# Linear attention into a two-layer network: k's maxima from a second copy of k with heads on the partitions, spread through DRAM

## The chip, the cores and the metric

The kernel runs on one core of one Trainium2 chip. The metric is the device time of one execution in microseconds (us). The engines are PE (TensorE, matmuls), ACT (ScalarE), DVE (VectorE), POOL (GpSimd) and SP (SyncE, which issues all DMAs here). Each works through its own instructions in order and waits for the others by semaphores.

## The reference

q, k and v have the shape 8 (batch) x 8 (heads) x 576 (positions) x 64. k's softmax runs over the positions, q's over the 64 elements of a row; the result, 4608 rows of 512, goes through a network with a hidden width of 2048. All is float32.

```python
q_s = np.exp(q - np.max(q, axis=-1, keepdims=True))
q_s = q_s / (np.sum(q_s, axis=-1, keepdims=True) + 1e-09)
k_s = np.exp(k - np.max(k, axis=2, keepdims=True))
k_s = k_s / (np.sum(k_s, axis=2, keepdims=True) + 1e-09)
kv = np.einsum('bhsd,bhse->bhde', k_s, v)
attn = np.einsum('bhsd,bhde->bhse', q_s, kv)
...
h = x @ w_in
g = np.where(h >= 1, h, np.where(h <= -1, 0.0, (h + 1) ** 2 / 4))
return g @ w_out
```

## The kernel before, in words

**Tiling.** The 4608 rows are worked in nine chunks of 512 rows (c); batch b's k and v are prepared in the stage of the same number. Heads go in four pairs (pr) of 2 x 64 = 128; two pairs make a half (h). The hidden width is cut into 16 blocks of 128 (f). A main matmul multiplies 128 x 128 weights with 128 x 512; each product of the network is three of them, from high and low parts of both factors. The first layer (h, L1446) runs block by block for chunks 0 to 2; chunks 3 to 8 go two at a time through seven products for four blocks (hA, hb, hC, L1505). The second layer (o, L1659) adds into one PSUM bank for each quarter of the chunk's rows. Between the two, ACT and DVE form g (relu L1596, square L1600, minimum L1605) and its parts gh (L1643) and gl (L1648).

**Attention.** Batches 0 and 1 (function attention) read k with the heads' elements on the partitions (in_kt, tiles kt or k of 128 x 576), so that a maximum over positions is one reduction along the free axis (L952). Batches 2 to 7 (attention_two, both halves: twelve stages) read k with positions on the partitions (in_k, 128 x 5 x 128), as kv_mms needs it. There the maximum runs across partitions:

- k_max (L1213): DVE reduces each pair's five rows per partition to m, 128 x 128, one per pair
- k_tr (L1221): PE transposes m into the tile mt in PSUM bank a, twice
- k_top (L1227): DVE reduces the two transposed tiles to mx, 128 x 2
- k_spread (L1232): PE transposes each column of mx, broadcast, back into mt, so that each partition holds all 128 maxima, twice
- k_sub (L1242): DVE subtracts mt from k; bank a is held until here
- k_exp (L1248) on ACT, then kv_mms (L1258), 40 matmuls on PE, kv_z and kv_f, which leave k's normalised product with v in kvt. x_two (L839) multiplies the transposed q with kvt to form the chunk's x.

**Order.** The kernel does not issue work as it is written. Each operation is noted in a plan with its engine, an estimated duration, a due time and what it waits for; tile buffers are handed on by rings, in which a taker waits until the earlier tile's readers are done. k's tiles have two rooms (for half 0 the tag k, for half 1 the tag st1). Plan.settle makes a first order by due times, then tries random moves of operations, one for each number in TURNS, and keeps an order unless Plan.play, a model of the engines with those durations, says that it is longer. The instructions are then recorded in that order, each on its engine. Loads and stores share SP's queue, in which a load that waits for a store's landing holds what stands behind it.

Of the kernel before, what the change touches and what calls it, by code (L numbers as in the profile page):

```python
# [13 lines left out]
F32 = mybir.dt.float32  # L14
# [64 lines left out]
class Op:  # L79
# [4 lines left out]
    def __init__(self, engine, us, due, emit, deps, port, kb, slack, other=()):  # L84
        self.engine, self.us, self.due, self.emit = engine, us, due, emit
        self.port, self.kb, self.slack = port, kb, slack
        self.ways = ((engine, us, port), *other)
        self.deps, self.users = deps, []
        self.missing = len(deps)
        self.ready = self.after = 0.0  # L90
        self.store = False
        self.margin = 0.8 if kb else 0.0
        self.wire = kb / 330
        for d in deps:
            d.users.append(self)
# [19 lines left out]
class Plan:  # L115
# [79 lines left out]
    )  # L195

    CASES, LATE = 3, 1.6

# [288 lines left out]
def tile_linear_attention_then_ffn(  # L487
# [414 lines left out]
    def attention(c, pr, due, step, slack):  # L902
# [163 lines left out]
        if not first:  # L1066
            rpk.take(mm)
# [842 lines left out]
```

## Time and profile before

| | us |
|---|---|
| three timed runs | 845.15, 844.44, 845.61 |
| median | 845.15 |
| the profiled execution's own time | 844.76 |
| its span, from the first to the last instruction | 843.0 |
| PE busy in it | 828.4 |
| first main matmul starts | 20.65 |

The profile is of one execution. A row of a group gives line, engine, operation, output <- inputs, shapes, count, then the busy time of the group, the mean duration in ns of one instruction, and the idle time of the engine just before them with what ended it. PEld are PE's weight loads, which overlap its matmuls. A DMA row gives the issues, the size of one and the median time from issue to landing. In the timeline and the chain the first two columns are start and duration.

### The profile page before, as it was taken

To read this page: it belongs to the slowest core of one execution; us is meant where nothing else is said; L and a number is where in the kernel's file an instruction comes from. 1 tells how busy PE (TensorE), PEld (TensorE's weight loads), DVE (VectorE), ACT (ScalarE), POOL (GpSimd) and SP (SyncE) were. 2 spreads that over 40 slices of the span, in tenths; PEclk is the share of its full clock that TensorE was granted. 3 is DMA by queue.
4 is the path that set the end of the run, shared out by engine and by line. 5 is a ranking of instruction groups with operands and counts; after the bars stand their busy time and mean duration, and the time that the engine had idled before them with its cause. 6 is when DMAs were issued, how large, how long until landed. Compare 5 with 4: busy or idle time off the path is not lost.

```text
span 843.0 us, 12228 instructions
## 1 busy us (share of the span) xinstructions
PE 828.4 (98%) x4364; PEld 663.6 (79%) x4364; DVE 457.3 (54%) x853; ACT 442.5 (52%) x758; POOL 329.1 (39%) x291
## 2 busy tenths in 40 slices
PE   8899999999999999999999999999999999999998
PEld 6587778877777787877877888787778888888786
DVE  6887774566756656776754315765641034545300
ACT  6787756443466454644656445554574245444522
POOL 4664555552446756200217691102157600000153
PEclk9999999999999999999999999999999999999999
DMA  9898865457578566766675536556465254544232
GB/s 338 274 318 294 290 218 213 145 165 241 193 258 274 173 217 224 246 215 228 194 248 206 153 99 194 195 193 210 145 216 178 76 187 138 175 138 162 75 102 87
DMA packets 65580, 166.38 MB, mean 197 GB/s; under 512 B 7280, under 2 KB 7536, under 8 KB 65520
## 3 DMA queue, kind: packets, MB, share of 16 engines
q1 hardware_dynamic: 65520, 165.61, 58.7%
q8 instruction: 34, 0.56, 0.3%
q14 instruction: 26, 0.21, 0.1%
HBM read 122.06 MB, written 43.52 MB: 196 GB/s over the span
## 4 chain that ended last, share of the span: by engine, by line
PE 93%; DVE 2%; ACT 2%; issue 1%; POOL 1%; DMA 1%; POOLq 0%; ACTq 0%
PE o L1659 45%; PE h L1446 16%; PE hA L1505 15%; PE hC L1505 8%; PE hb L1505 4%; PE x L839 2%; PE kv L1258 2%; PE warm L1841 1%; PE kv L988 1%; DMA out<-osb 1%; DVE qmo L1345 0%; ACT r L1596 0%; PE ep L963 0%; ACT osb L533 0%; PE tp L1035 0%
## 5 line engine op out<-in xcount | busy, mean ns | idle before, releaser
L1659 PE MATMUL o<-wl,gh 128*128 128x512 f32 x576 | 227.8, 396 | 0.3 <-ACT osb L533 0.3
L1659 PE MATMUL o<-wh,gl 128*128 128x512 f32 x576 | 224.9, 390 | 0.1
L1659 PE MATMUL o<-wh,gh 128*128 128x512 f32 x576 | 224.4, 390 | 0.0
L1505 PE MATMUL hA<-x,w 128*128 128x512 f32 x576 | 145.8, 392 | 1.6 <-ACT sn_P L533 1.2
L1659 PEld LDWEIGHTS o<-wl,gh 128*128 128x128 f32 x576 | 108.1, 188 | 26.8 <-issue 3.6
L1659 PEld LDWEIGHTS o<-wh,gl 128*128 128x128 f32 x576 | 108.1, 188 | 24.9 <-POOL gl L1648 1.0
L1505 PEld LDWEIGHTS hA<-x,w 128*128 128x128 f32 x576 | 107.2, 188 | 26.0 <-ACT sn_P L533 1.8
L1659 PEld LDWEIGHTS o<-wh,gh 128*128 128x128 f32 x576 | 108.2, 188 | 21.4
L1446 PE MATMUL h<-x,w 128*128 128x512 f32 x432 | 110.1, 396 | 2.2 <-DVE gl L1648 1.5
L1446 PEld LDWEIGHTS h<-x,w 128*128 128x128 f32 x432 | 79.3, 188 | 23.0 <-DVE gl L1648 2.1
L1600 ACT ACTIVATE r<-r 128x512 f32<-128x512 f32 x139 | 87.8, 633 | 3.8
L1505 PE MATMUL hC<-x,w 128*128 128x512 f32 x288 | 73.9, 392 | 0.1
L1596 ACT ACTIVATE r<-c,half 128x512 f32<-128x512 f32 x48 | 34.7, 723 | 68.2 <-DVE c L1529 68.1
L1648 POOL TENSOR_TENSOR gl<-gs,gh 128x512 fp32r<-128x512 f32 x42 | 54.2, 1291 | 41.7 <-ACT gh L1643 41.1
L1354 POOL TENSOR_TENSOR q<-q,qzb 128x512 f32<-128x512 f32 x28 | 28.9, 1050 | 105.3 <-DVE qzb L1376 91.0
L1354 POOL TENSOR_TENSOR q<-q,qmb 128x512 f32<-128x512 f32 x28 | 28.8, 1049 | 100.9 <-DVE qmb L1346 100.9
L1154 POOL TENSOR_TENSOR x<-xc,x 128x512 fp32r<-128x512 f32 x40 | 51.8, 1307 | 35.9 <-ACT x L1149 35.9
L1643 ACT CAST gh<-gs 128x512 fp32r<-128x512 f32 x42 | 26.1, 622 | 73.2 <-PE o L1659 63.4
L1505 PEld LDWEIGHTS hC<-x,w 128*128 128x128 f32 x288 | 53.6, 188 | 12.3 <-DVE sn_P L535 0.5
L1596 ACT ACTIVATE r<-h,half 128x512 f32<-128x512 f32 x48 | 33.0, 687 | 52.2 <-PE h L1446 51.9
L1648 POOL TENSOR_TENSOR gl<-c,gh 128x512 fp32r<-128x512 f32 x6 | 7.8, 1294 | 126.9 <-ACT gh L1643 126.8
L1605 DVE SCALAR_TENSOR_TENSOR h<-h,r 128x512 f32<-128x512 f32 x48 | 33.1, 694 | 37.1 <-ACT r L1600 34.0
(123 smaller groups left out, 1176.3 us busy)
## 6 DMA issues: line engine op xcount, KB each, us to landing
w<-b SPq DMA_DIRECT2D x50, 512.0 KB, 4.5
w<-s SPq DMA_DIRECT2D x48, 512.0 KB, 3.5
st<-in_w SPq DMA_DIRECT2D x32, 512.0 KB, 6.2
g<-c SPq DMA_DIRECT2D x42, 256.0 KB, 4.1
gs<-g SPq DMA_DIRECT2D x42, 256.0 KB, 2.6
v<-in_v SPq DMA_DIRECT2D x32, 325.0 KB, 4.9
q<-in_q SPq DMA_DIRECT2D x36, 256.0 KB, 3.7
out<-osb SPq DMA_DIRECT2D x35, 256.0 KB, 2.5
```

The lines of the kernel that those rows point to most:

```text
L839: nc.tensor.matmul(t[r][cols, :, p0:p1], kvt[rows, g % NKV, pr, :], q[pr]["tq"][rows, :, p0:p1], start=True, stop=True, tile_position=(r * ...
L1154: eng.tensor_tensor(x[:, 1, :], t["xc"][:, at, :], f32(x[:, 0, :]), ALU.subtract)
L1258: nc.tensor.matmul(kv[d, i, :], t[pr]["k"][:, j, d], t[pr]["v"][:, j, e * (D + 1) : (e + 1) * (D + 1)], start=(j == 0), stop=(j == KJ - 1) ...
L1354: nc.gpsimd.tensor_tensor(qf, qf, at, alu)
L1446: nc.tensor.matmul(t["h"], lhs, rhs, start=(turn == 0 and i == 0), stop=(turn == NPAIR - 1 and i == 2),)
L1505: nc.tensor.matmul(banks[b]["h"], lhs, rhs, start=(begins and not kk and not m), stop=(ends and kk == 1 and m == 2), skip_group_check=True,)
L1596: nc.scalar.activation(t["r"], t["h"], AF.Relu, bias=half[:, :1], scale=0.5)
L1600: nc.scalar.activation(t["r"], t["r"], AF.Square)
L1605: nc.vector.scalar_tensor_tensor(t["h"], t["h"], 1.0, t["r"], ALU.max, ALU.min)
L1643: nc.scalar.copy(t["gh"], t["h"])
L1648: eng.tensor_tensor(t["gl"], t["h"], f32(t["gh"]), ALU.subtract)
L1659: nc.tensor.matmul(outs[c, j], lhs[:, s], rhs, start=(begins and i == 0), stop=(closes and i == 2),)
```

## The change

In the twelve stages of attention_two the maxima of k come from a second copy of k. in_kt, which held batches 0 and 1, now holds all eight, in the layout with heads on the partitions. For each pair a stage loads its 128 x 576 copy into one of k's rooms, DVE reduces it along the free axis to a column of mx (128 x 2), and the copy's room is free again. mx is stored to a small DRAM tensor mk, 2 x 128, element by element, and loaded back as one row of 256 that goes to all 128 partitions of m2. k_sub subtracts this tile from k, which is loaded as before. k_tr, k_top and k_spread, with their four transposes on PE and the hold on PSUM bank a, are gone.

The planner gets a mode for each PE operation (0 main matmuls, 1 x_two, 2 the kv products, 3 transposes); its model adds 0.1 when the mode changes, and the estimates of x_two and kv_mms are lower by 0.1 and 0.09. The numbers in TURNS are others. Lines after the change are smaller by 16 to 22: L1483 stands for L1505, L1637 for L1659, L1234 for L1258.

```diff
     TURNS = (
-        10001, 10002, 10003, 10011, 10013, 10026, 10029, 10031, 10033, 10036, 10041, 10042,
...
+        2, 3, 4, 12, 18, 19, 20, 21, 25, 27, 30, 31, 34, 35, 37, 39, 41, 43, 44, 46, 47, 49, 51,
...
+            if e == "PE" and op.mode != mode:
+                t, mode = t + 0.1, op.mode
...
-        xm = do("PE", 1.05, due, x_mm, *ready, *deps)
+        xm = do("PE", 0.95, due, x_mm, *ready, *deps)
+        xm.mode = 1
...
         def k_max(i):
             def emit():
                 if not i:
-                    b["m"] = wk.tile([P, 2, P], F32, tag="m2", name=f"m2_{n}")
-                k = t[two[i]]["k"].rearrange("p j d -> p d j")
-                nc.vector.tensor_reduce(b["m"][:, i, :], k, AX.X, ALU.max)
...
+                    b["mx"] = sm.tile([P, 32], F32, tag="mx", name=f"mx_{n}", bufs=1)
+                kt_ = t[two[i]]["kt"].rearrange("p j s -> p (j s)")
+                nc.vector.tensor_reduce(b["mx"][:, i : i + 1], kt_, AX.X, ALU.max)
...
+        def m_store():
+            nc.sync.dma_start(maxima.rearrange("i p -> p i"), b["mx"][:, :2])
+
+        def m_load():
+            b["m"] = wk.tile([P, 2, P], F32, tag="m2", name=f"m2_{n}")
+            nc.sync.dma_start(
+                b["m"].rearrange("p i d -> p (i d)"),
+                maxima.rearrange("i p -> (i p)").unsqueeze(0).broadcast_to([P, 2 * P]),
+            )
...
-                mb = t[pr]["mb"].unsqueeze(1).broadcast_to([P, KJ, P])
+                mb = b["m"][:, pr % 2, :].unsqueeze(1).broadcast_to([P, KJ, P])
                 nc.vector.tensor_tensor(k, k, mb, ALU.subtract)
...
+            maxima = dp.tile([2, P], F32, name=f"mk{n}")
+            rx, rm = ring("sm mx", 1), ring("wk m2", 1)
+            tops, before = [], rx.wait()
             for i, pr in enumerate(two):
+                lk, rk = load(pr, "kt", kt[c, pr], [P, 1, S], 288, kdue - 14 + 3 * i, tag)
+                km = do("DVE", 0.75, kdue - 12 + 3 * i, k_max(i), lk, *before)
+                rk.free(km)
...
+            out_ = plan.save(0.45, kdue - 6, m_store, tops, 64)
+            rx.free(out_)
+            spread = plan.read(0.45, kdue - 2, m_load, [out_, *rm.wait()], 128)
+            rm.take(spread)
...
+                subs.append(do("DVE", 0.9, kdue + 14, k_sub(pr), lk, spread, port=True))
...
-            one = do("PE", 0.13, kdue + 8, k_tr(0), loads[two[0], "m"], *ra.wait())
-            ra.take(one)
-            other = do("PE", 0.13, kdue + 8, k_tr(1), loads[two[1], "m"], one)
-            top = do("DVE", 0.4, kdue + 10, k_top, one, other)
-            rm.free(top)
-            spread = [do("PE", 0.13, kdue + 12, k_spread(i), top) for i in range(2)]
-            subs = [do("DVE", 0.81, kdue + 14, k_sub(pr), *spread) for pr in two]
-            ra.free(*subs)
...
-            mm = do("PE", 1.34, at, kv_mms, *exps, *deps, *ra.wait())
+            mm = do("PE", 1.25, at, kv_mms, *exps, *deps, *ra.wait())
+            mm.mode = 2
```

Three places show how the instructions move; all belong to chunk 6, half 0. In a row stand line, operation, output <- inputs, shape and a repeat count; the last number in a name only counts tiles.

PE before, in the first products of chunks 3 and 4 (hb, hC) beside the last second-layer block of chunk 2 (o_2, block 15): the transposes are mt.

```order
L1505 MATMUL hb_3_0_3560<-x3_3517,w_3_0_0_3401 128x512 x3
L1659 MATMUL o_2_1_2749<-wl15_1030,gh_2_15_3525 128x512
L1659 MATMUL o_2_1_2749<-wh15_1029,gh_2_15_3525 128x512
L1659 MATMUL o_2_1_2749<-wh15_1029,gl_2_15_3536 128x512
L1221 MATMUL mt_6_0_3575<-ident_95,m2_6_0_3547 128x128 x2
L1505 MATMUL hC_3_0_3583<-x6_2973,w_3_0_1_3407 128x512 x3
L1505 MATMUL hC_3_0_3583<-x7_3549,w_3_0_1_3407 128x512 x3
L1659 MATMUL o_2_2_2740<-wl15_1030,gh_2_15_3525 128x512
L1659 MATMUL o_2_2_2740<-wh15_1029,gh_2_15_3525 128x512
L1659 MATMUL o_2_2_2740<-wh15_1029,gl_2_15_3536 128x512
L1232 MATMUL mt_6_0_3575<-ident_95,mx_6_0_3592 128x128 x2
L1659 MATMUL o_2_3_2764<-wl15_1030,gh_2_15_3525 128x512
```

PE now, at the same work:

```order
L1637 MATMUL o_2_1_2751<-wl15_1047,gh_2_15_3543 128x512
L1637 MATMUL o_2_1_2751<-wh15_1046,gh_2_15_3543 128x512
L1637 MATMUL o_2_1_2751<-wh15_1046,gl_2_15_3550 128x512
L1483 MATMUL hA_3_0_3578<-x0_2730,w_3_0_0_3469 128x512 x3
L1483 MATMUL hA_3_0_3578<-x1_3563,w_3_0_0_3469 128x512 x3
L1234 MATMUL kv_6_0_3592<-v_6_0_3341,k_6_0_3384 64x65 x10
L1234 MATMUL kv_6_0_3592<-v_6_1_3348,k_6_1_3402 64x65 x10
L1483 MATMUL hb_3_0_3622<-x2_2778,w_3_0_0_3469 128x512 x3
L1483 MATMUL hb_3_0_3622<-x3_3576,w_3_0_0_3469 128x512 x3
```

The two pairs of transposes are gone, and the kv products, which stood 14 rows behind the second pair before, now stand among these products.

DVE before, the same stage: L1213 are the maxima of k, L1227 k_top, L1242 the subtractions.

```order
L1213 TENSOR_REDUCE m2_6_0_3547<-k_6_0_3489 128x128
L1213 TENSOR_REDUCE m2_6_0_3547<-k_6_1_3493 128x128
L1529 TENSOR_TENSOR hb_3_0_3560<-hb_3_0_3560,sn_P1_3_0_3542 128x512
L1334 TENSOR_REDUCE qa_6_0_3436<-q_6_1_3498 128x16
L1227 TENSOR_REDUCE mx_6_0_3592<-mt_6_0_3575 128x2
L1605 SCALAR_TENSOR_TENSOR hb_3_0_3560<-hb_3_0_3560,r_3_0_3581 128x512
L535 COPY osb_2_1_3601<-o_2_1_2749 128x512
L1648 TENSOR_TENSOR gl_3_0_3613<-hb_3_0_3560,gh_3_0_3603 128x512
L1345 COPY qmo_6_0_3617<-qa_6_0_3436 32x32 x4
L1346 TENSOR_TENSOR qmb_6_0_3618<-qa_6_0_3436,qmo_6_0_3617 128x32
L1242 TENSOR_TENSOR k_6_0_3489<-k_6_0_3489,mt_6_0_3575 128x640
L1242 TENSOR_TENSOR k_6_1_3493<-k_6_1_3493,mt_6_0_3575 128x640
```

DVE now, from the second maximum (L1200) to what stands behind the subtractions (L1218); L1583 is the minimum, L1626 gl, L742 a split of summed weights:

```order
L1200 TENSOR_REDUCE mx_6_0_3376<-kt_6_1_3325 128x1
L1353 TENSOR_SCALAR qzb_5_0_3364<-qzb_5_0_3364 128x32
L1354 RECIPROCAL qzb_5_0_3364<-qzb_5_0_3364 128x32
L1583 SCALAR_TENSOR_TENSOR h_2_12_3397<-h_2_12_3397,r_2_12_3418 128x512
L1200 TENSOR_REDUCE mx_5_1_3439<-kt_5_2_2954 128x1
L1626 TENSOR_TENSOR gl_2_12_3449<-h_2_12_3397,gh_2_12_3441 128x512
L742 TENSOR_TENSOR w_s_7_0_3447<-ss_7_3420,w_s_7_0_3447 128x2x256
L1583 SCALAR_TENSOR_TENSOR h_2_13_3359<-h_2_13_3359,r_2_13_3432 128x512
L1218 TENSOR_TENSOR k_6_0_3384<-k_6_0_3384,m2_6_0_3426 128x640
L1218 TENSOR_TENSOR k_6_1_3402<-k_6_1_3402,m2_6_0_3426 128x640
L1583 SCALAR_TENSOR_TENSOR h_2_14_3353<-h_2_14_3353,r_2_14_3467 128x512
L1626 TENSOR_TENSOR gl_2_13_3503<-h_2_13_3359,gh_2_13_3496 128x512
```

The stage has moved ahead, to the last blocks of chunk 2; seven instructions now stand between the second maximum and the subtraction that waits for the load.

SP before, the stage's loads beside weight fetches (w_3) and stores (out):

```order
L1201 DMA k_6_0_3489<-in_k 128x640
L1201 DMA k_6_1_3493<-in_k 128x640
L1201 DMA q_6_1_3498<-in_q 128x512
L676 DMA w_3_0_3_3509<-b1_113 128x512
L1201 DMA v_6_0_3511<-in_v 128x650
L1201 DMA v_6_1_3519<-in_v 128x650
L1717 DMA out<-osb_2_0_3557 128x512
```

SP now, from the second copy's load; mk is the store of the maxima, m2 their load:

```order
L1188 DMA kt_6_1_3325<-in_kt 128x576
L658 DMA w_2_15_3336<-b15_127 128x1024
L1188 DMA v_6_0_3341<-in_v 128x650
L1188 DMA v_6_1_3348<-in_v 128x650
L1188 DMA k_6_0_3384<-in_k 128x640
L1205 DMA mk6_0_175<-mx_6_0_3376 128x2x1
L856 DMA xk4_3_173<-xo_4_3_3395 128x512
L1188 DMA k_6_1_3402<-in_k 128x640
L1209 DMA m2_6_0_3426<-mk6_0_175 128x256
L1188 DMA k_5_2_3451<-in_k 128x640
L750 DMA s7_0_142<-w_s_7_0_3447 128x1024
L658 DMA w_3_0_0_3469<-b0_112 128x1024
```

Between the store and the load of the maxima stand two other DMAs; the fetches of the next weights stand behind the load.

More of the change, by code (lines that the diff above doesn't have):

```diff
@@ L93, in __init__ @@
         self.wire = kb / 330
+        self.mode = 0
         for d in deps:
@@ L323, in play @@
         ends, gaps, why = {}, [], {}
+        mode = 0
         for op in order:
@@ L1052, in attention @@
         tr = do("PE", 0.6, 2, kt_tr, ke, *rpk.wait(), *(et.wait() * first))
+        tr.mode = 3
         rpk.take(tr)
@@ L1059, in attention @@
             tr = do("PE", 0.25, 2.7, kt_tr2, ke, *rpk.wait())
+            tr.mode = 3
             rk.free(tr)
@@ L1084, in attention @@
         tr = do("PE", 0.45, 3.6, q_tr, qn, *rpq.wait())
+        tr.mode = 3
         rpq.take(tr)
@@ L1210, in emit @@
                 if not i:
-                    b["m"] = wk.tile([P, 2, P], F32, tag="m2", name=f"m2_{n}")
-                k = t[two[i]]["k"].rearrange("p j d -> p d j")
-                nc.vector.tensor_reduce(b["m"][:, i, :], k, AX.X, ALU.max)
-            return emit
-        def k_tr(i):
-            def emit():
-                if not i:
-                    b["mt"] = ps_a.tile([P, 4, P], F32, tag="a", name=f"mt_{n}")
-                nc.tensor.transpose(b["mt"][:, i, :], b["m"][:, i, :], ident)
-            return emit
-        def k_top():
-            b["mx"] = sm.tile([P, 32], F32, tag="mx", name=f"mx_{n}", bufs=1)
-            nc.vector.tensor_reduce(b["mx"][:, :2], b["mt"][:, 0:2, :], AX.X, ALU.max)
-        def k_spread(i):
-            def emit():
-                t[two[i]]["mb"] = b["mt"][:, 2 + i, :]
-                nc.tensor.transpose(
-                    t[two[i]]["mb"], b["mx"][:, i : i + 1].broadcast_to([P, P]), ident
-                )
-            return emit
+                    b["mx"] = sm.tile([P, 32], F32, tag="mx", name=f"mx_{n}", bufs=1)
+                kt_ = t[two[i]]["kt"].rearrange("p j s -> p (j s)")
+                nc.vector.tensor_reduce(b["mx"][:, i : i + 1], kt_, AX.X, ALU.max)
+            return emit
+        def m_store():
[6 more added lines that the diff above has]
+            )
         def k_sub(pr):
@@ L1278, in attention_two @@
         if c < NB:
-            rm = ring("wk m2", 1)
-            loads, rooms, maxed = {}, {}, rm.wait()
-            for i, pr in enumerate(two):
-                tag = ("k", "st1")[h]
-                loads[pr, "k"], rooms[pr, "k"] = load(
-                    pr, "k", k[c - KT, pr], [P, KJ, P], 320, kdue + 6 * i, tag
+            loads, rooms = {}, {}
+            tag = ("k", "st1")[h]
+            maxima = dp.tile([2, P], F32, name=f"mk{n}")
+            rx, rm = ring("sm mx", 1), ring("wk m2", 1)
+            tops, before = [], rx.wait()
+            for i, pr in enumerate(two):
+                lk, rk = load(pr, "kt", kt[c, pr], [P, 1, S], 288, kdue - 14 + 3 * i, tag)
+                km = do("DVE", 0.75, kdue - 12 + 3 * i, k_max(i), lk, *before)
+                rk.free(km)
+                tops.append(km)
+                if not i:
+                    rx.take(km)
+                before = [km]
+            out_ = plan.save(0.45, kdue - 6, m_store, tops, 64)
+            rx.free(out_)
+            spread = plan.read(0.45, kdue - 2, m_load, [out_, *rm.wait()], 128)
+            rm.take(spread)
+            subs, exps = [], []
+            for i, pr in enumerate(two):
+                lk, rooms[pr, "k"] = load(
+                    pr, "k", k[c - KT, pr], [P, KJ, P], 320, kdue + 10 + 6 * i, tag
                 )
@@ L1288, in attention_two @@
                 )
-            for i, pr in enumerate(two):
-                km = do("DVE", 1.3, kdue + 6 * i, k_max(i), loads[pr, "k"], *maxed, port=True)
-                maxed = [km]
-                if not i:
-                    rm.take(km)
-                loads[pr, "m"] = km
-            exps = []
-            ra = ring("ps a", 1)
-            one = do("PE", 0.13, kdue + 8, k_tr(0), loads[two[0], "m"], *ra.wait())
-            ra.take(one)
-            other = do("PE", 0.13, kdue + 8, k_tr(1), loads[two[1], "m"], one)
-            top = do("DVE", 0.4, kdue + 10, k_top, one, other)
-            rm.free(top)
-            spread = [do("PE", 0.13, kdue + 12, k_spread(i), top) for i in range(2)]
-            subs = [do("DVE", 0.81, kdue + 14, k_sub(pr), *spread) for pr in two]
-            ra.free(*subs)
+                subs.append(do("DVE", 0.9, kdue + 14, k_sub(pr), lk, spread, port=True))
+            rm.free(*subs)
             exps = [do("ACT", 0.74, kdue + 20 + 12 * i, k_exp(pr), subs[i]) for i, pr in enumerate(two)]
@@ L1308, in attention_two @@
             deps = [loads[pr, "v"] for pr in two]
-            mm = do("PE", 1.34, at, kv_mms, *exps, *deps, *ra.wait())
+            mm = do("PE", 1.25, at, kv_mms, *exps, *deps, *ra.wait())
+            mm.mode = 2
             ra.take(mm)
@@ L1870 @@
     kk = rows(inputs["k"]).transpose(0, 1, 3, 4, 2, 5).reshape(b, NPAIR, P, 2 * KJ * D)
-    kt = rows(inputs["k"])[:KT].transpose(0, 1, 2, 5, 4, 3).reshape(KT, NPAIR, P, KJ * P)
+    kt = rows(inputs["k"]).transpose(0, 1, 2, 5, 4, 3).reshape(b, NPAIR, P, KJ * P)
     kt = kt[..., :S]
```

116 rows, old and new, of the table TURNS are left out of this document.

## The prediction

> **What bounds the kernel now.** I read the page first: its busy shares and its chain.
>
> ```profile
> span 843.0 us, 12228 instructions
> PE 828.4 (98%) x4364; PEld 663.6 (79%) x4364; DVE 457.3 (54%) x853; ACT 442.5 (52%) x758; POOL 329.1 (39%) x291
> ...
> PE 93%; DVE 2%; ACT 2%; issue 1%; POOL 1%; DMA 1%; POOLq 0%; ACTq 0%
> ```
>
> TensorE (PE) is busy in 98% of the span, and 93% of the chain that ended last is its work. The other engines stand idle 46% of the time or more. So a change is worth what it takes out of PE's row of instructions or out of PE's waits, and costs what it adds to either. Work on DVE, SP or the DMA engines counts only where PE comes to wait for it.
>
> Next the busy times by stage (start and end, length, PE busy with its count, then PEld, DVE, ACT, POOL, clock, DMA share, GB/s):
>
> ```profile
> 20.00:104.00 84.00, 80.36 (x436) 62.01 (x431) 66.90 (x122) 64.13 (x116) 48.95 (x39) 1.00 0.87 294
> 104.00:312.00 208.00, 205.82 (x1195) 164.22 (x1194) 129.94 (x260) 106.48 (x185) 111.09 (x107) 1.00 0.61 206
> 312.00:632.00 320.00, 317.77 (x1667) 253.57 (x1667) 185.81 (x344) 173.12 (x291) 108.16 (x92) 1.00 0.60 200
> ```
>
> The twelve stages that the change touches lie in the last two of these rows, and the clock stands at its full 1.00. PE idles there for 208.00 - 205.82 + 320.00 - 317.77 = 4.4 us in all. That is all that better timing could win there; the rest must come from fewer instructions. PE's waits between 95 and 570 us, where the twelve stages lie, all of them (total, times, longest):
>
> ```profile
> PE h L1446 <- DVE gl L1648: 1.5, 1, 1.5
> PE hA L1505 <- ACT sn_P L533: 1.2, 1, 1.2
> PE kv L1258 <- ACT k L1248: 0.9, 2, 0.7
> PE o L1659 <- ACT osb L533: 0.3, 1, 0.3
> ```
>
> One row is on the path that the change replaces: kv_mms waited 0.9 us for the exponential of k. No row names a DMA. That matters below, because the change moves the maxima from PE to DMAs.
>
> **What the transposes cost on PE.** They are these two groups, 48 instructions:
>
> ```profile
> L1221 PE MATMUL mt<-ident,m 128*128 128x128 f32 x24 | 4.9, 271 | 0.0
> L1232 PE MATMUL mt<-ident,mx 128*128 128x128 f32 x24 | 4.7, 272 | 0.0
> ```
>
> Their busy time is no price, since matmuls overlap in the pipeline; I take it from starts. An undisturbed run of main matmuls gives the step:
>
> ```profile
> 143.06 5.44 PE o L1659 x24
> ```
>
> 24 matmuls in 5.44 us, so 0.227 us from start to start. Now a pair of transposes in PE's timeline, and then one standing alone (start, duration):
>
> ```profile
> 117.69 1.53 PE L1446 MATMUL h<-x,w 128*128 128x512 f32 x6
> 119.06 0.38 PE L1221 MATMUL mt<-ident,m 128*128 128x128 f32 x2
> 119.19 0.48 PE L1659 MATMUL o<-wl,gh 128*128 128x512 f32 x1
> 119.51 0.39 PE L1659 MATMUL o<-wh,gh 128*128 128x512 f32 x1
> 119.74 0.40 PE L1659 MATMUL o<-wh,gl 128*128 128x512 f32 x1
> 119.97 0.85 PE L1446 MATMUL h<-x,x 128*128 128x512 f32 x3
> ...
> 153.78 0.85 PE L1446 MATMUL h<-x,x 128*128 128x512 f32 x3
> 154.46 0.27 PE L1221 MATMUL mt<-ident,m 128*128 128x128 f32 x1
> 154.49 0.94 PE L1446 MATMUL h<-x,w 128*128 128x512 f32 x3
> 155.27 0.85 PE L1446 MATMUL h<-x,x 128*128 128x512 f32 x3
> ```
>
> From 117.69 to 119.97 stand 6 + 3 = 9 main matmuls, which need 9 x 0.227 = 2.04 us; they took 2.28. The pair costs 0.24: about 0.14 before the next main matmul starts, and 0.09 because the one after it comes 0.32 instead of 0.227 later. From 153.78 to 155.27 stand 6 main matmuls, 1.36 us; they took 1.49, so a lone transpose costs 0.13. Part of the price is thus for leaving and re-entering the main matmuls, not for the transpose.
>
> **The change part by part.** *Transposes removed.* In the order before, the 48 stand as 21 pairs and 6 alone, each time between main matmuls; afterwards there are none. 21 x 0.24 + 6 x 0.13 = **5.8 us** off PE. Nothing hides this; PE is the engine that is never free.
>
> *Planner's mode count.* PE's main matmuls are interrupted in 72 places before and 44 after: 27 fewer by the transposes above, and one more because two remaining transposes now stand together. That one is worth the re-entry, 0.09: **0.1 us**. The new costs (1.25 for 1.34, 0.95 for 1.05) are numbers in the plan; the 20 matmuls per pair of heads, and all other PE work, stay.
>
> *DVE.* Rows for it:
>
> ```profile
> L1213 DVE TENSOR_REDUCE m<-k 128x128 f32<-128x640 f32 x24 | 30.8, 1302 | 0.0
> L1227 DVE TENSOR_REDUCE mx<-mt 128x2 f32<-128x256 f32 x12 | 5.1, 421 | 10.0 <-PE mt L1221 10.0
> L1242 DVE TENSOR_TENSOR k<-k,mt 128x640 f32<-128x640 f32 x24 | 18.7, 815 | 13.5 <-PE mt L1232 13.5
> L952 DVE TENSOR_REDUCE nm<-kt 128x1 f32<-128x576 f32 x4 | 2.9, 737 | 3.9 <-DMA kt<-in_kt 3.9
> ```
>
> The 24 maxima of k fall from 1.30 to about 0.74 each (the same reduction of the same shape in the last row): 30.8 - 17.8 = 13.0 us. The 12 second maxima go, 5.1 us. The subtraction keeps its shape, but its second operand moves from PSUM to SBUF. Operands of 128x512 take 0.692 us in the first row below (one in PSUM) and 0.687 in the second (both in SBUF), so I leave it at 0.815:
>
> ```profile
> L1529 DVE TENSOR_TENSOR c<-hC,sn_P 128x512 f32<-128x512 f32 x24 | 16.6, 692 | 52.1 <-PE hC L1505 48.3 <-ACT sn_P L533 2.8 <-ACT q L1361 1.1
> L1154 DVE TENSOR_TENSOR x<-xc,x 128x512 fp32r<-128x512 f32 x2 | 1.4, 687 | 2.7 <-ACT x L1149 2.7
> ```
>
> DVE loses 18 us of 457, worth nothing directly, since it was idle nearly half the time. For the kv wait it is worth between 0 and 0.9 us; I take **0.5**, half of that row, as the path is renewed and no row of it remains.
>
> *Loads added.* 24 loads of 288 KB and, with rows of 128 x 256, twelve of 128 KB: 8.4 MB more in the 528 us of two stages that move 206 and 200 GB/s, 107 MB: about 8%, or 5 points of their DMA share of 0.61 and 0.60. The copies take the rooms of k, two at a time, so each k is loaded only after a copy's maximum; its landing runs beside the round trip. The first six copies fall where the share is 0.87, before and just after 104 us. Cost 0 while PE waits for no DMA; if that cover went, each load ahead of a weight load would delay it by about 1 us (288 KB at 294 GB/s).
>
> *The wait added.* The maxima go to DRAM in pieces of 4 bytes and come back to all partitions; the load is issued on SP only when the store has landed. No such store is in the trace. The rows nearest to a store and a load by SP:
>
> ```profile
> xk<-xo SPq DMA_DIRECT2D x24, 256.0 KB, 4.0
> xc<-xk SPq DMA_DIRECT2D x24, 256.0 KB, 3.3
> ...
> b<-w SPq DMA_DIRECT2D x10, 512.0 KB, 6.9
> ...
> out<-osb SPq DMA_DIRECT2D x2, 128.0 KB, 2.0
> ```
>
> Low end of the round trip: twice the fastest row, 2.0 + 2.0 = 4.0 us. The closest pair by what it does is xk and xc, 4.0 + 3.3 = 7.3. High end: 6.9 + 3.3 = 10.2. I take 5.0, since 1 KB is stored and 128 KB loaded, nearer to the last row than to 256 KB. Two things queue behind it. On SP stand weight fetches and stores behind the waiting load; it holds them for the store's landing, 2 to 4 us, twelve times. That is nothing new on SP, whose loads of xk wait for their own stores in the same way (seven waits, up to 3.4 us):
>
> ```profile
> SPq L1122 <- DMA xk<-xo: 9.6, 7, 3.4
> ```
>
> PE has no wait on a DMA all the same: cost 0, and if that cover went, up to the 4 us of one landing. On DVE the subtraction waits for the load, and behind it stand the products that PE needs (for chunk 6, half 0: the min for block 14 and gl of block 13). Between the second maximum and the first subtraction stand in the new order 7 DVE instructions for chunk 6 half 0, 10 each for chunk 2 half 0 and chunk 4 half 0, and 13 to 32 in the other nine. The seven are a maximum (0.74), four of 128x512 (0.69 by the row above) and two small ones, for which I take this row:
>
> ```profile
> L1376 DVE RECIPROCAL qzb<-qzb 128x32 f32<-128x32 f32 x14 | 4.9, 353 | 0.5
> ```
>
> 0.74 + 4 x 0.69 + 2 x 0.35 = 4.2 us of DVE work. Ten make at most 6.9, with a few small ones about 6.5; thirteen 9.0. DVE was busy only 0.62 and 0.58 of the two stages, so the time that passes is nearer to 7, 10.5 and 15. A trip of 5.0 fits everywhere but, if DVE never idles there, in the first place (0.8 late). I take 0.
>
> The Trainium skill speaks against this store: by DMA: Bandwidth & Descriptors, section Specifications, pieces under 512 B are not moved at line rate but with a read-modify-write. It gives no duration for 4-byte pieces, and no row here shows any. If the rule made the trip as long as the high end, the slower case below would apply; if the fixed landing time rules, the sum stands.
>
> *The rest of the order.* The list of kept turns is another, so every engine's order is drawn anew, in the first 20 us too. The idle time of the first row of stages, 84.00 - 80.36 = 3.6 us, and the 4.4 above may each shrink or grow. I take 0 and keep plus or minus 4.
>
> **The sum.** -5.8 - 0.1 - 0.5 = -6.4 us. The profiled execution took 844.76 (span 843.0 and 1.8 around it), so 838.4 for such an execution. It lay 0.39 under the median of the runs shown, 845.15; against that median the time is 838.75, rounded **838.8**.
>
> **Rivals.** *More comes back than the transposes.* With 18 us less on DVE and PSUM bank a no longer held from the first transpose to the subtraction, the waits of the middle stages vanish too: 838.8 + 0.5 - 4.4 = 834.9. For it speaks that the long DVE waits in the rows above (10.0 and 13.5 us on mt) go; against it that three of PE's four waits there have nothing to do with k. Chance 0.13 for under 836.
>
> *The transposes were cover, or the new order waits elsewhere.* The change then takes the instructions out but PE waits for the same gl or x a little later. If the drawn order adds half of what PE idles in the three rows (3.6 + 4.4 = 8.0), that gives 838.8 + 4.0 = 842.8; with all of it again, 846.8. For it speaks that the order is drawn anew as a whole; against it that after the transposes shown, the main matmuls went on with no idle time. Chance 0.12 for 843.5 to 846.8.
>
> *The round trip is late (the slower side).* Mechanism: DVE stands at the subtraction of chunk 6 half 0, chunk 2 half 0 and chunk 4 half 0, and PE behind gl. With no idle time on DVE in between, a trip of 7.3 us is late by 3.1 + 0.8 + 0.8 = 4.7 (843.5); of 8.4 by 4.2 + 1.9 + 1.9 = 8.0 (846.8), from which it is slower; of 10.2, with two of the rest at 9.0, by 6.0 + 3.7 + 3.7 + 1.2 + 1.2 = 15.8 (854.6). Against it: the elapsed time between is longer than DVE's busy time, and PE usually has matmuls of an earlier block left. Chance 0.09 for above 846.8.
>
> The Trainium skill (TensorE: Matmul & The Clock Gate, section on HAM oscillation) adds that PE idle for more than about 3.4 us falls back to half clock; the longest wait of PE in these stages is 1.5 us, at a clock of 1.00, so no run shows it, and only the slower case would reach it.
>
> **How the numbers follow.** The forecast, 836 to 843.5, has 0.66; more 0.13; given back 0.12; late 0.09. What a measurement of this kernel can tell from no change is 0.2%, 1.7 us: faster means under 843.5, 0.66 + 0.13 = 0.79; the same 0.12; slower 0.09. The range runs from 834.5, just past the case in which the middle stages' waits vanish, to 845.0, where half of the cases that give the saving back are in; that leaves out about 0.04 below and 0.15 above. The round trip's high end, 854.6, lies beyond it.
>
> **What would show it.** PE's busy time should fall by 5 to 6 us with the mt groups gone, and the middle stages' idle time stay near 4.4. The longest transfer of the pair, from the store's issue to the load's landing, should be near 5 us, and DVE should show little wait for a DMA at the subtraction. A row in which PE waits for gl, min or kv behind such a wait, or in which PE waits for a weight fetch, would prove me wrong; so would a first main matmul later than before by more than 2 us.

## The result and the profile after

The changed kernel takes 875.27 us (median of four runs, 870.26 to 878.88); the kernel before, run at the same time, took 845.38 (844.44 to 846.11). The ratio is 1.035, with a 95% interval of 1.030 to 1.040: **slower by 30 us**, where 838.8 was predicted and 845.0 was the upper end of the range. The profiled execution is the longest of the four, 878.88, with a span of 877.1 us.

The page of the changed kernel (busy time, share of the span, instructions; then the granted clock, the share of its full speed that PE's clock was given, in tenths for 40 slices, 9 for 90% or more; then the packets):

```profile
span 877.1 us, 12241 instructions
PE 839.4 (96%) x4316; PEld 670.0 (76%) x4316; DVE 451.2 (51%) x847; ACT 446.0 (51%) x755; POOL 329.7 (38%) x288
PEclk9899999899899999999999999999999999999999
DMA packets 74030, 175.06 MB, mean 200 GB/s; under 512 B 11120, under 2 KB 12912, under 8 KB 73968
```

PE has 48 instructions fewer, as planned, and yet is busy 11 us longer, at a mean clock of 0.980 where it was 1.00. Its idle time has grown as well: 877.1 - 839.4 = 37.7 us, where it was 843.0 - 828.4 = 14.6. The windows of the same stages as before say where:

```profile
20.00:104.00 84.00, 78.19 (x413) 60.80 (x410) 64.94 (x120) 63.08 (x113) 44.49 (x36) 0.96 0.84 280
104.00:312.00 208.00, 189.62 (x1050) 148.25 (x1049) 112.26 (x229) 93.07 (x160) 94.13 (x90) 0.95 0.73 206
312.00:632.00 320.00, 313.59 (x1624) 250.98 (x1623) 183.75 (x350) 169.51 (x282) 116.39 (x99) 0.99 0.70 212
```

In the second row PE idles 18.4 us of 208 where it idled 2.2, and does 1050 matmuls where it did 1195. The DMA engines are busy for 0.73 of the time where it was 0.61, and move the same 206 GB/s: more time for the same bytes. The DMA rows (size of one, median us from issue to landing) tell which; first the changed kernel's, then the same rows before:

```profile
w<-b SPq DMA_DIRECT2D x50, 512.0 KB, 5.6
out<-osb SPq DMA_DIRECT2D x35, 256.0 KB, 3.9
s<-w_s SPq DMA_DIRECT2D x16, 512.0 KB, 7.3
k<-in_k SPq DMA_DIRECT2D x24, 320.0 KB, 8.5
mk<-mx SPq DMA_DIRECT2D x12, 1.0 KB, 9.8
m<-mk SPq DMA_DIRECT2D x12, 128.0 KB, 4.9
```

```profile
w<-b SPq DMA_DIRECT2D x50, 512.0 KB, 4.5
out<-osb SPq DMA_DIRECT2D x35, 256.0 KB, 2.5
s<-w_s SPq DMA_DIRECT2D x16, 512.0 KB, 4.3
k<-in_k SPq DMA_DIRECT2D x24, 320.0 KB, 4.7
```

The store of 1 KB is the slowest transfer of the list, 9.8 us, and transfers that have nothing to do with it land later than before: k 8.5 for 4.7, s 7.3 for 4.3. How much of that is the store's and how much the new order's, these rows don't tell; the first experiment does. Two explanations of the loss offer themselves. The waits for the round trip are there (total, times, longest; the last two are SP's):

```profile
DVE k L1218 <- DMA m<-mk: 24.6, 6, 8.5
DVE osb L517 <- DMA out<-osb: 14.9, 2, 12.1
DVE mx L1200 <- DMA mk<-mx: 11.0, 3, 6.4
SPq L1209 <- DMA mk<-mx: 57.1, 8, 8.5
```

DVE stands at the subtraction for 24.6 us and SP at the load for 57.1; the longest single wait of DVE, 12.1, is for an ordinary store of results. On PE the waits are spread thin, over many releasers, none of them for m or mk:

```profile
PE h L1424 <- DVE gl L1626: 4.3, 3, 1.9
PE kv L1234 <- DVE x L843: 3.8, 1, 3.8
PE o L1637 <- DVE gl L1626: 3.5, 3, 2.3
PE o L1637 <- DVE osb L517: 3.4, 1, 3.4
PE h L1424 <- DMA w<-b: 3.1, 1, 3.1
```

What follows such a wait is the second half of the loss. In PE's timeline (start, duration; the wait in brackets) after the one of 2.29 us:

```profile
218.13 0.39 PE L1637 MATMUL o<-wh,gh 128*128 128x512 f32 x1
220.81 0.50 PE L1637 MATMUL o<-wh,gl 128*128 128x512 f32 x1 [2.29 <-DVE gl L1626]
...
221.45 0.63 PE L1637 MATMUL o<-wh,gh 128*128 128x512 f32 x1
221.87 0.63 PE L1637 MATMUL o<-wh,gl 128*128 128x512 f32 x1
...
224.01 0.63 PE L1637 MATMUL o<-wh,gh 128*128 128x512 f32 x1
224.43 0.53 PE L1637 MATMUL o<-wh,gl 128*128 128x512 f32 x1
```

The step from start to start is 0.43 us instead of 0.227 for about 3.4 us: half clock (the granted clock of this trace is 0.50 from 222.00 to 224.60 us). The wait was paid, and then some 1.7 us more.

### The profile page after: what moved, and what is told of

The parts are those of the page before. It is cut to its first block, busy times and chain, and to the rows that moved or that the text cites. A ratio compares the mean times of both kernels' runs of the same rounds, so it can differ in the third digit from the quotient of the medians.

```text
span 877.1 us, 12241 instructions
## 1 busy us (share of the span) xinstructions
PE 839.4 (96%) x4316; PEld 670.0 (76%) x4316; DVE 451.2 (51%) x847; ACT 446.0 (51%) x755; POOL 329.7 (38%) x288
## 5 line engine op out<-in xcount | busy, mean ns | idle before, releaser
L1637 PE MATMUL o<-wl,gh 128*128 128x512 f32 x576 | 230.5, 400 | 7.0 <-DVE osb L517 3.4
L1637 PE MATMUL o<-wh,gl 128*128 128x512 f32 x576 | 227.4, 395 | 3.6 <-DVE gl L1626 3.5
L1637 PE MATMUL o<-wh,gh 128*128 128x512 f32 x576 | 227.0, 394 | 0.0
L1483 PE MATMUL hA<-x,w 128*128 128x512 f32 x576 | 145.8, 393 | 3.1 <-DVE c L1507 2.8
L1637 PEld LDWEIGHTS o<-wl,gh 128*128 128x128 f32 x576 | 109.6, 190 | 36.9 <-issue 4.7
L1637 PEld LDWEIGHTS o<-wh,gl 128*128 128x128 f32 x576 | 109.7, 190 | 29.1 <-DVE gl L1626 5.2
L1483 PEld LDWEIGHTS hA<-x,w 128*128 128x128 f32 x576 | 107.8, 188 | 27.8 <-DVE c L1507 5.0
L1637 PEld LDWEIGHTS o<-wh,gh 128*128 128x128 f32 x576 | 109.8, 191 | 21.9
L1424 PE MATMUL h<-x,w 128*128 128x512 f32 x432 | 113.3, 410 | 10.1 <-DVE gl L1626 4.3
L1424 PEld LDWEIGHTS h<-x,w 128*128 128x128 f32 x432 | 84.2, 198 | 32.3 <-DVE gl L1626 5.6
L1483 PE MATMUL hC<-x,w 128*128 128x512 f32 x288 | 73.5, 391 | 0.0
L1141 POOL TENSOR_TENSOR x<-xc,x 128x512 fp32r<-128x512 f32 x41 | 54.0, 1327 | 43.0 <-ACT x L1136 43.0
L1626 POOL TENSOR_TENSOR gl<-gs,gh 128x512 fp32r<-128x512 f32 x42 | 54.2, 1290 | 37.0 <-ACT gh L1621 34.4
L1483 PEld LDWEIGHTS hC<-x,w 128*128 128x128 f32 x288 | 53.8, 188 | 12.3 <-ACT sn_P L515 0.8
L1626 POOL TENSOR_TENSOR gl<-c,gh 128x512 fp32r<-128x512 f32 x5 | 6.4, 1288 | 121.8 <-PE o L1637 117.8
L1583 DVE SCALAR_TENSOR_TENSOR h<-h,r 128x512 f32<-128x512 f32 x48 | 33.2, 692 | 29.9 <-ACT r L1578 29.7
```

The costliest lines, as they stand in the source:

```text
L1141: eng.tensor_tensor(x[:, 1, :], t["xc"][:, at, :], f32(x[:, 0, :]), ALU.subtract)
L1424: nc.tensor.matmul(t["h"], lhs, rhs, start=(turn == 0 and i == 0), stop=(turn == NPAIR - 1 and i == 2),)
L1483: nc.tensor.matmul(banks[b]["h"], lhs, rhs, start=(begins and not kk and not m), stop=(ends and kk == 1 and m == 2), skip_group_check=True,)
L1583: nc.vector.scalar_tensor_tensor(t["h"], t["h"], 1.0, t["r"], ALU.max, ALU.min)
L1626: eng.tensor_tensor(t["gl"], t["h"], f32(t["gh"]), ALU.subtract)
L1637: nc.tensor.matmul(outs[c, j], lhs[:, s], rhs, start=(begins and i == 0), stop=(closes and i == 2),)
```

## The experiments

Three theories. **A**: the trip is late, and DVE and SP, which wait for it, hold up others. **B**: the store of 4-byte pieces slows every other transfer while it lands, whoever waits for it. **C**: the new order, or the 24 copies of k, cost it by themselves.

### Taking the trip out: e1_no_trip

```diff
 def m_store():
-    nc.sync.dma_start(maxima.rearrange("i p -> p i"), b["mx"][:, :2])
+    pass
 def m_load():
-    (tile m2 and its load)
+    b["m"] = ones
```

> The changed kernel, same order, without the store and the load of the maxima; the subtraction takes a constant tile, so k is shifted by 1 instead of by its maxima (the normalised product is the same in exact arithmetic). The maxima are still reduced from the second copies. Theory A (the round trip is late: its store lands 9.8 us after issue, DVE waits 24.6 us for it, SP 57 us) and theory B (the 4-byte pieces hold up the other DMAs) both expect the sum of the prediction, 836 to 842 us. Theory C (the new order and the 24 added copies cost by themselves) expects more than 855.

Measured: 837.22 us (835.45 to 839.35), ratio 0.990 (0.988 to 0.992). C falls: order, copies and maxima on DVE together are worth -8.7 us against 845.94 of the kernel before, run at the same time (so it is with "beside it" below). All that was lost, 38 us against the changed kernel, hangs on the trip.

This trace also puts the rows above right. Without the trip s still lands in 6.8 us, w (512 KB) in 5.2 and out in 3.7, nearly as late as in the changed kernel, and it costs nothing: most of that comes with the new order and the copies. What the trip adds is k's 8.5 us for 4.8, and a lower rate: from 104 to 312 us the DMA engines move 236 GB/s at a busy share of 0.69 without the trip, 206 at 0.73 with it.

### The store alone, in the kernel before: e2_store_4B and e2b_store_128B

```diff
-b["mx"] = sm.tile([P, 32], F32, tag="mx", name=f"mx_{n}", bufs=1)
+b["mx"] = sm.tile([P, 32], F32, tag="mx", name=f"mx_{n}", bufs=12)
 nc.vector.tensor_reduce(b["mx"][:, :2], b["mt"][:, 0:2, :], AX.X, ALU.max)
+mk = dp.tile([2, P], F32, name=f"mk{n}")
+nc.sync.dma_start(mk.rearrange("i p -> p i"), b["mx"][:, :2])
```

> The kernel before, same order, with a store of its maxima (128 x 2, pieces of 4 bytes, as in the changed kernel) added behind each of the twelve second maxima; nothing reads it. Theory A expects 845 to 848 us, since nobody waits for the store. Theory B expects a large part of the loss, 855 to 870, with other DMAs landing later around the stores. In both the store itself should land about 9 us after its issue.

The control stores the whole mx, 128 pieces of 128 bytes, and clears it first with one DVE instruction per stage:

> The same as the run before it with a store of 128 pieces of 128 bytes (16 KB) in place of 256 pieces of 4 bytes. It is the control for SP's wait for the second maximum. Theories A and B both expect 845 to 848 us and a landing of 2 to 4 us; if it lands as late as the 4-byte store, the size of the pieces is not the cause.

Measured: 892.26 us (881.85 to 893.65), ratio 1.052 (1.046 to 1.058), with the 4-byte pieces; 851.15 (850.58 to 851.54), ratio 1.0065 (1.005 to 1.008), with the 128-byte pieces. Both lie above what either theory expected; the control's 5 us are explained further down. Nobody reads either store, and with twelve buffers for mx the program makes nobody wait for its landing. The rows of the first run, then of the second:

```profile
s<-w_s SPq DMA_DIRECT2D x16, 512.0 KB, 7.9
k<-in_k SPq DMA_DIRECT2D x24, 320.0 KB, 6.3
mk<-mx SPq DMA_DIRECT2D x12, 1.0 KB, 10.1
```

```profile
s<-w_s SPq DMA_DIRECT2D x16, 512.0 KB, 4.7
k<-in_k SPq DMA_DIRECT2D x24, 320.0 KB, 4.9
mk<-mx SPq DMA_DIRECT2D x12, 16.0 KB, 1.6
```

Sixteen times the bytes land in a sixth of the time, and the neighbours are left nearly alone (s 4.3 and k 4.7 in the kernel before). Here the order is the same in both runs, so the difference is the store's. Medians hide the worst of it. For xk, which passes x between chunks through DRAM, these are the landings of its stores and loads in the kernel before, with the packed store, and with the same pieces 64 bytes apart (e10 below):

```profile
DMA to landing us min/median/max: 2.0/3.7/7.0
```

```profile
DMA to landing us min/median/max: 2.0/4.3/15.6
```

```profile
DMA to landing us min/median/max: 2.0/3.4/6.7
```

SP's waits for the stores of xk grow from 9.6 us to 47.8. The profile puts two more waits of SP, 6.3 us, down to mk, at loads of xc that the program doesn't make wait for it. B is thus enough to make the loss without anybody waiting for the trip by the program.

### The store in the changed order, without its readers: e6_store_unread

The edit is e1_no_trip's with the store left in.

> The changed kernel with its 4-byte store, but without the load: the subtraction takes a constant tile of ones (so the output's attention is computed with another shift of k), and nobody waits for the store's landing. It tells the two theories apart inside the changed order. If the changed kernel is slow because DVE stands at the subtraction and SP at the load, this run is near the one without the trip, 837 us, at most 841. If the store is dear because other transfers are held up while it lands, most of the 38 us stays: 860 to 875 us, with k's loads again near 8 us and stretches at half clock.

Measured: 878.70 us (872.74 to 884.45), ratio 1.039 (1.033 to 1.044); the changed kernel's 1.035 (1.030 to 1.040) cannot be told from it, and the time is a little above the 860 to 875 expected. The load and the wait at the subtraction add nothing that can be measured. One wait for the store is left in this kernel, since mx has a single buffer:

```profile
DVE mx L1201 <- DMA mk<-mx: 17.5, 4, 8.1
DVE k L1215 <- DMA k<-in_k: 4.9, 3, 3.4
```

So A is not excluded to the last microsecond; but with none of A's waits at the subtraction and at the load the whole loss is there, and so it is in e2_store_4B, where the program has no wait for the store at all.

### What makes the store slow: e4, e5, e7, e10

All are e2_store_4B with another shape of the stored tile, as e4's edit shows:

```diff
-mk = dp.tile([2, P], F32, name=f"mk{n}")
-nc.sync.dma_start(mk.rearrange("i p -> p i"), b["mx"][:, :2])
+mk = dp.tile([2, P, P], F32, name=f"mk{n}")
+nc.sync.dma_start(mk[:, :, 0].rearrange("i p -> p i"), b["mx"][:, :2])
```

> The kernel before, with a store of mx behind each k_top that nobody reads: 256 pieces of 4 bytes as in the run with the packed store, but each piece goes to a place of its own in DRAM, 512 bytes from the next. If the pieces are slow because they are small, whatever they hit, the store again takes about 10 us to land and the time is near that run's 892 us. If they are slow because the 16 DMA engines write into the same few hundred bytes and wait for each other, the store lands in about 2 us (the store of 128 pieces of 128 bytes landed in 1.6 us) and the time is near that run's 851 us.

> The kernel before, with an unread store of the same 1 KB behind each k_top, as 128 pieces of 8 bytes, packed in DRAM. If the price goes with the number of pieces, landing falls to about half of 10.1 us, 5 us, and the time is between 851 and 892 us, near 870; if it goes with the bytes or with the DRAM region, landing stays near 10 us and the time near 892; if 8 bytes are already free of it, landing is near 1.6 us and the time near 851.

> The kernel before, with an unread store of one column of mx alone behind each k_top: 128 pieces of 4 bytes, 512 bytes in all (the second column of maxima is not stored). If the price goes with the number of pieces, landing is about half of 10.1 us, 5 us, as with 128 pieces of 8 bytes, and the time near 870 us. If it went with the bytes, this store would land sooner than the one of 128 pieces of 8 bytes.

> The kernel before with the unread store of 256 pieces of 4 bytes, now 64 bytes apart in DRAM, and eleven buffers for mx in place of twelve (a move of 1280 bytes, a whole multiple of 256, in place of 1408). If pieces wait for each other only within a line of at most 64 bytes, the store lands in about 2 us, as at 512 bytes apart; if the line is longer, it lands later, between 2 and 10 us. By the reading that the move by an odd multiple of 128 bytes cost 5 us, a landing of 2 us goes with a time of 845 to 846.5 us; if the moves cost nothing, with 850 to 852.

Measured, with the two stores above; the landing is the median of the row mk<-mx in each trace, and the fourth column is worked out from the shape:

| run | pieces | apart | pieces in 64 bytes of DRAM | landing, us | time, us | ratio (interval) |
|---|---|---|---|---|---|---|
| e2_store_4B | 256 of 4 B | 4 B | 16 | 10.1 | 892.26 | 1.052 (1.046 to 1.058) |
| e7_store_half | 128 of 4 B | 4 B | 16 | 8.9 | 878.99 | 1.040 (1.037 to 1.044) |
| e5_store_8B | 128 of 8 B | 8 B | 8 | 4.1 | 856.43 | 1.012 (1.010 to 1.014) |
| e4_store_4B_apart | 256 of 4 B | 512 B | 1 | 2.0 | 850.33 | 1.0055 (1.0035 to 1.008) |
| e10_store_4B_64 | 256 of 4 B | 64 B | 1 | 1.9 | 846.13 | 1.000 (0.999 to 1.001) |
| e2b_store_128B | 128 of 128 B | 128 B | 1 or fewer | 1.6 | 851.15 | 1.0065 (1.005 to 1.008) |

Here are the rows of e10, e5 and e7, each from its own trace:

```profile
mk<-mx SPq DMA_DIRECT2D x12, 1.0 KB, 1.9
```

```profile
mk<-mx SPq DMA_DIRECT2D x12, 1.0 KB, 4.1
```

```profile
mk<-mx SPq DMA_DIRECT2D x12, 0.5 KB, 8.9
```

Neither size nor number of pieces decides by itself: 256 pieces of 4 bytes land in 1.9 us when they lie 64 bytes apart, as fast as pieces of 128 bytes. The expectation that 128 pieces would take half the time of 256, if the number decides, failed as well: 8.9 for 10.1, while 128 pieces of 8 bytes, fewer to each 64 bytes, took 4.1. In these six stores the landing goes with how many pieces hit the same small region of DRAM. Among the packed ones (4 and 8 bytes) the size of a piece changes along with that number, so that step alone would not tell them apart; the stores with pieces apart do. Which unit makes the pieces wait for each other, and how large the region is, these runs don't tell; 64 bytes apart is enough.

### A second effect: where the weights lie: e9_shift_128B

e4 and e2b cost about 5 us although their stores land in 2 us, and e10, with eleven buffers for mx in place of twelve, costs nothing. One edit of the kernel before tests it:

```diff
-b["mx"] = sm.tile([P, 32], F32, tag="mx", name=f"mx_{n}", bufs=1)
+b["mx"] = sm.tile([P, 32], F32, tag="mx", name=f"mx_{n}", bufs=2)
```

> The kernel before with a second buffer of 128 bytes for mx and nothing else changed: no store, no new instruction. If the move of what lies behind it in SBUF by 128 bytes slows the second layer's matmuls by 2.5 ns each, the time is 849 to 851 us, as with the two unread stores that landed within 2 us (851.2 and 850.3), and those stores then cost next to nothing. If the stores were what cost 5 us there, this run is at 845.4.

Measured: 850.11 us (849.99 to 850.44), ratio 1.005 (1.003 to 1.007), with not one instruction added. PE's groups of the second layer, before and then in e9 (busy us, mean ns of one):

```profile
L1659 PE MATMUL o<-wl,gh 128*128 128x512 f32 x576 | 227.8, 396 | 0.3 <-ACT osb L533 0.3
L1659 PE MATMUL o<-wh,gl 128*128 128x512 f32 x576 | 224.9, 390 | 0.1
L1659 PE MATMUL o<-wh,gh 128*128 128x512 f32 x576 | 224.4, 390 | 0.0
```

```profile
L1659 PE MATMUL o<-wl,gh 128*128 128x512 f32 x576 | 229.2, 398 | 0.4 <-ACT osb L533 0.4
L1659 PE MATMUL o<-wh,gl 128*128 128x512 f32 x576 | 226.5, 393 | 0.1
L1659 PE MATMUL o<-wh,gh 128*128 128x512 f32 x576 | 225.5, 392 | 0.0
```

Each is 2 to 3 ns longer, 1.4 + 1.6 + 1.1 = 4.1 us in all. That is the difference from the runs beside it (850.11 - 846.14 = 4.0) and most of the 5.2 us between the spans of these two traces (848.2 and 843.0). The pool of mx lies ahead of the one that holds second-layer weights, so a bigger mx moves these. Moves of 128 and 11 x 128 = 1408 bytes slowed the second layer; a move of 10 x 128 = 1280 did not (nor did 256, below). That fits a cost at odd multiples of 128 bytes; why there is one was not tried. It means that the unread stores with short landings cost next to nothing themselves (850.33 and 851.15 against 850.11), and that of e2's loss 892.26 - 850.11 = 42 us are the packed store's.

### The trip without packed pieces: e3_store_128B and e8_store_128B_pad

DVE turns mx by its 32 x 32 transpose, so that each partition that is stored holds 32 maxima in a row:

```diff
+nc.vector.memset(b["mx"], 0.0)
 nc.vector.tensor_reduce(b["mx"][:, i : i + 1], kt_, AX.X, ALU.max)
+if i:
+    b["mxt"] = sm.tile([P, 32], F32, tag="mxt", name=f"mxt_{n}", bufs=1)
+    nc.vector.transpose(b["mxt"], b["mx"])
...
-nc.sync.dma_start(maxima.rearrange("i p -> p i"), b["mx"][:, :2])
+rows = b["mxt"].rearrange("(g r) c -> r g c", g=4)
+for i in range(2):
+    nc.sync.dma_start(maxima[i].rearrange("(g c) -> g c", g=4), rows[i])
```

> The changed kernel, same order, with the maxima turned on DVE (a 32x32 transpose of a 128x32 tile) so that the store goes out as 8 pieces of 128 bytes (two DMAs) instead of 256 of 4. Theories A and B expect the store to land in 2 to 4 us and 838 to 848 us in all. Theory C expects more than 855.

Measured: 841.59 us (840.88 to 842.17), ratio 0.995 (0.9935 to 0.9965). The second layer's matmuls were longer here too, as in e9, so the new tile was widened to 64 columns:

> The changed kernel with its maxima turned by a DVE transpose and stored in pieces of 128 bytes, as in the run at 841.6 us, but with the new tile 64 columns wide in place of 32, so that what lies behind it in SBUF moves by 256 bytes and not by 128; only 32 columns are used. In that run the second layer's matmuls stepped at 229.4 to 230.2 ns in place of 227.1 to 227.3 without the trip, which makes up 5.5 of the 6.7 us between the two spans. If this comes from where the second layer's weights lie (a move by 128 bytes), the step goes back to 227 and the time is 836.5 to 838.5 us. If it comes from the trip itself (its loads, the SP time, the transposes), the time stays at 841 to 842.5 us.

Measured: 836.66 us (835.78 to 838.48), ratio 0.989 (0.988 to 0.991): **the whole change, with its round trip, 9.5 us faster than before**, and as fast as without the trip. Its page, DVE's wait at the subtraction and a second-layer group:

```profile
span 836.7 us, 12283 instructions
PE 822.3 (98%) x4316; PEld 659.9 (79%) x4316; DVE 458.2 (55%) x871; ACT 445.0 (53%) x755; POOL 329.2 (39%) x288
...
L1643 PE MATMUL o<-wl,gh 128*128 128x512 f32 x576 | 227.1, 394 | 0.5 <-ACT gh L1627 0.5
```

```profile
DVE k L1224 <- DMA m<-mk: 1.3, 2, 1.1
```

Beside this run the changed kernel's loss can be added up. Its span is 877.1 - 836.7 = 40.4 us longer: PE idles 37.7 instead of 14.4, 23.3 us more, and is busy 839.4 instead of 822.3 with the same 4316 matmuls, 17.1 us more. The latter is the half clock: a mean clock of 0.980 means about 0.020 x 877.1 / 0.5 = 35 us at half speed (0.998 here: 3), and what runs then takes twice as long.

### The planner's mode count: e11_no_mode

```diff
-                t, mode = t + 0.1, op.mode
+                t, mode = t, op.mode
```

> The kernel with pieces of 128 bytes and the wider tile, with the planner's added 0.1 for a change of mode set to 0: another order of the same instructions, with the same list of turns. The prediction valued the mode count at 0.1 us by itself and the redrawn order at 0 plus or minus 4. If that holds, the time is within 4 us of the run with the mode count beside it; if the list of turns works only with the count, it is over 4 us slower.

Measured: 842.05 us (839.85 to 846.18), ratio 0.995 (0.994 to 0.997), 5.4 above the same kernel with the count. Without the count the same list of turns gives another order, and this one is slower, by more than the 4 us that the expectation allowed; no other was tried.

## Why the prediction was wrong

- **What bounds the kernel, and the transposes (-5.8, -0.1):** right. With the same 48 instructions gone and no packed store, PE's busy time fell from 828.4 to 822.3, 6.1 us (e8_store_128B_pad). The 0.1 is too small to be seen alone.
- **The wait at kv (-0.5), the copies and their loads (0), DVE's lighter work (0):** right as a whole. e1_no_trip has all of them and took 837.22; e8_store_128B_pad, with the trip, 836.66. The forecast of 838.8 described these kernels within 2.2 us. The closeness is in part luck. The saving against the kernel before beside them was 8.7 and 9.5 us, where the sum had 6.4. And in e8's trace PE idles 0.5 us in the two middle rows of stages, where it idled 4.4, as the rival "more comes back" had it, but 6.3 in the first, where it idled 3.6; the sum had put both at 0, and they nearly cancel. PE's lists of waits in both traces have no row for kv any more.
- **The round trip, 5.0 us between 4.0 and 10.2:** wrong in size. The store landed in 9.8 us (8.4 to 12.6) and the load in 4.9, together 14.7, above the upper end. The bounds came from the fastest and slowest of the large transfers, as if a small one could not be slower than a big one.
- **The cost of the trip, 0:** this is the step that failed. It asked only who waits for the trip, and that PE had no wait for a DMA was read as cover. The sum had no term for what the store does to the other transfers, and that is where the loss of 38 us comes from: e2_store_4B loses 42 us with nobody made to wait for the store, e6_store_unread has it without load and wait at the subtraction, and e10_store_4B_64, the same pieces 64 bytes apart, has none of it.
- **The rival "the round trip is late"** had the sign, with 854.6 at most, but not the mechanism: its waits do exist (24.6 us on DVE, 57.1 on SP), yet without those two the time is the same (e6_store_unread, 878.70 us). It also named gl as what PE would wait for; three of PE's five longest rows name something else, since any transfer may be the one that comes late.
- **The Trainium skill's rule on pieces under 512 B** (DMA: Bandwidth & Descriptors, Specifications), which the prediction set beside this store, points at the right place. By the size alone it would have made pieces of 4 bytes dear at any distance and those of 128 bytes too; at 64 bytes apart they landed in 1.9 us and at 128 bytes long in 1.6, so here the packing decided.
- **The clock.** The prediction left out half clock, since no wait before was long enough. Once transfers came late it made up about 17 of the 40 us, and a wait of 2.29 us was already followed by it. The Trainium skill (TensorE: Matmul & The Clock Gate, HAM oscillation) puts the limit at idle time above about 3.4 us. The trace does not agree with that, and the measurement decides.
- **The rest of the order, 0 plus or minus 4:** the drawn order cost nothing (e1_no_trip); the one other order that was tried cost 5.4 us, somewhat more than the 4 allowed.

## What to carry to other kernels

A transfer has two prices, what waits for it and what it does to the transfers beside it; a tiny store that scatters words side by side into DRAM can be dear in the second although nobody waits for it, so spread its pieces (which helped here in an unread store) or turn them into rows first (which made this change pay). No row of a big transfer bounds such a store: where the trace shows none of its kind, leave the range open above. When a control differs from its base in more than the edit, here in the size of a buffer, measure that difference alone before reading the control.

## What was not expected of the hardware

- 256 pieces of 4 bytes, packed into 1 KB of DRAM, landed in 10.1 us, and 1.9 us when 64 bytes apart; with the packed store in the kernel, other transfers took up to about twice as long (k 8.5 us in the changed kernel, 4.8 without the trip; xk at most 15.6 us for 7.0).
- A wait of PE of 2.29 us was followed by about 3.4 us of matmuls at a step of 0.43 in place of 0.227 us.
- 128 more bytes in a pool ahead of the second layer's weights made each of its 1728 matmuls about 2 ns longer and the kernel 0.5% slower (850.11 us against 846.14 beside it); 256 bytes cost nothing that was seen (836.66 us, where 128 took 841.59).
